# A retention and expert-mixture kernel: other slots for the remainder, the second-half units and some loads of tile 0, and another order of the last head units

## The chip, the cores and the metric

The kernel runs on one core of one Trainium2 chip. The metric is the device time of one execution in microseconds. The five engines are named as in the profile: PE (TensorE, with PEld for its weight loads), DVE (VectorE), ACT (ScalarE), POOL (GpSimd) and SP (SyncE, which only issues DMAs here).

## The reference

First a causal linear attention (retention) with 8 batches, 8 heads, 576 positions, head size 64:

```python
scores = (1/sqrt(64)) * q @ k^T
Dmat[h, i, j] = gamma[h] ** (i - j)  if i >= j else 0
attn = (scores * Dmat) @ v                      # (8, 8, 576, 64)
x = attn.transpose(0, 2, 1, 3).reshape(4608, 512)
```

Then a mixture of 4 experts over the 4608 rows, D = 512, F = 1024:

```python
p = domain_probs / (domain_probs.sum(-1) + 1e-9)
out = sum over e of  p[:, e] * (relu(x @ w1[e]) @ w2[e])
```

## The kernel before

**The decay** is split into a factor on k and a factor on q, so that each attention step is: cast q, k, v to bf16 with the factors, transpose q and k, scores on PE, the triangular mask on DVE (`sT`), a running sum of k^T v for the earlier chunks (`kv` on PE, then `sbd`), and values: first the products of the own chunk (`v` with `sT`), then the carried products (`sbd` with q).

**Attention of batch 0** is done ahead of everything else, in four `Unit`s `us[0]` to `us[3]` (half of the 512 positions, half of the heads; units 0 and 1 give rows p = 0, 1 of `xt`, units 2 and 3 rows p = 2, 3). Their transposes run on PE (`trans_pe`, L503) and are copied by ACT (L505). `scores` is L526 on PE and L528 on DVE, `kv` L545 on PE and L564 on ACT, `values` L575 (own) and L582 (carried) on PE and L598 on ACT. `warm(n)` issues n products of zeros (L140) on PE.

**Tile 0** follows: the rows 0 to 511. Its experts are walked in turn, 4 groups of up products (`up_group`, L345, 8 matmuls of 128x512, Relu on ACT, L349) and 4 of down products (`down_plain`, L364, 8 matmuls; every second one is read by DVE, L374 or L376, into an accumulator `acc0` and, for the last expert, stored by SP). That is 32 groups, numbered 0 to 31. After group n the functions listed in `slots[n]` are issued, in the order in which they were added. Expert e has its up groups in slots 8e to 8e+3 and its down groups in 8e+4 to 8e+7.

In these slots stand the work of the coming tiles:

- `remainder(slots, 0, ...)`: positions 512 to 575 of batch 0 (`Rem`): cast on DVE (L307, L309), two DMA transposes on the SP queue (L318, `kTr`, `qTr`), scores (L324 on PE, L325 on DVE), values (L330, L332 on PE, L336 on ACT). They write tile 1's `xt`.
- four second-half units `vs[0]` to `vs[3]`, batch 1, again `Unit`s: `v_cast` casts k and q on DVE (L492) and v on ACT (L488) and issues two DMA transposes on SP (`trans_dma`, L511, into `qkT`); `v_head` is scores and kv; then values. `qkT` and `sT` have two buffers each (`atp`, `bufs=2`), so the transposes of unit 2 wait until unit 0's values have read theirs, and those of unit 3 for unit 1.
- loads on the SP queue: `load_p` (the mixing weights of tile 1, `pB`), `load_pair` (batch 2, first pair, `raw1`), `load_rem(1)` (remainder of batch 1, `rawr`).
- `w_sum(which, lo, hi)` on DVE (L385 to L391): sums of the w2 weights, used from tile 1 on, where a fast form of the down products needs 7 instead of 8 partial products. `which` 1 overwrites a part of `wx[0]`, the w2 of experts 0 and 1.

The weights and the raw q, k, v of the second-half units are loaded on POOL's queue in a fixed order: w1(0) in halves, w2(0), w1(1), w2(1), remainder, w1(2), w2(2), units 0 and 1, w1(3), unit 2, w2(3), and unit 3 from inside `v_cast(0)`. `raws[3]` is the same buffer as `raws[0]`. `wx` holds w2, `w` w1.

**Tiles 1 to 8** have 16 up groups and 14 products each, with the attention of batch t + 1 in the slots of tile t; the remainder of batch 1 is cast in slot 0 of tile 1.

**PSUM** is one ring of four buffers of two banks; each `ring_tile` takes a free one, and waits for the readers of what was in it. The order of the instructions on each engine is the order in which the program issues them. Every engine works its own queue in order, and so do the DMA queues' issuers.

Of the kernel before, what the change touches and what calls it, by code (L numbers as in the profile page):

```python
# [23 lines left out]
def kernel(  # L24
# [10 lines left out]
    nc = tc.nc  # L35
    B, H, S, D = q.shape
    N, E = moe_domain_probs.shape
# [3 lines left out]
    C = 128  # L41
# [24 lines left out]
    def ring_tile(name, shape, dt=FP32):  # L66
        return ring.tile(shape, dt, tag="ring", name=name)
# [5 lines left out]
    def load_pair(t, b, p, eng=nc.sync):  # L73
        for n, src in srcs:
            for j in range(2):
                eng.dma_start(out=t[n][:, :, j, :],
                              in_=src[b, 2 * p + j, 0:SM, :].rearrange("(c p) d -> p c d", p=C))

    def load_rem(b, eng=nc.sync):
        for j in range(2):  # L80
            for n, src in (("k", k), ("v", v)):
                eng.dma_start(out=rawr[n][64 * j:64 * j + 64, :, j, :],
                                  in_=src[b, j:H:2, SM:S, :].rearrange("g t d -> t g d"))
        eng.dma_start(out=rawr["q"][0:R, :, :, :].rearrange("t g j d -> t (g j) d"),
                          in_=q[b, :, SM:S, :].rearrange("h t d -> t h d"))
# [3 lines left out]
    raw1 = {n: const.tile([128, NC, 2, D], FP32, name=f"raw1_{n}") for n, _ in srcs}  # L89
# [11 lines left out]
    def load_w1(e, f=slice(0, F)):  # L101
        return nc.gpsimd.dma_start(out=w1_sb[e][:, :, f], in_=moe_w1[e][:, f].rearrange("(dc p) f -> p dc f", p=128))
# [10 lines left out]
    NU = 4  # L113
# [23 lines left out]
    def warm(n):  # L137
        w = ring_tile("w", [128, 512])
        for _ in range(n):
            nc.tensor.matmul(w, lhsT=zz[:, 0:128], rhs=zz, start=True, stop=True)  # L140
# [69 lines left out]
    def mixing_weights():  # L210
        nc.vector.tensor_reduce(psm, prb, axis=mybir.AxisListType.X, op=ADD)
        nc.vector.tensor_scalar_add(psm, psm, 1e-9)
        nc.vector.reciprocal(psm, psm)
        nc.vector.tensor_tensor(pn, prb[:, :, :].rearrange("p t e -> p e t"),
                                psm.unsqueeze(1).to_broadcast([128, E, NTT]), op=MULT)
        nc.sync.dma_start(out=pd[:, :].rearrange("e (p t) -> p e t", p=128), in_=pn)
# [3 lines left out]
    def load_p(t, e, eng):  # L220
        pB[t, e] = ppool.tile([128, NT], FP32, tag="pB", name="pB")
        eng.dma_start(out=pB[t, e], in_=pd[e:e + 1, t * NT:(t + 1) * NT].to_broadcast([128, NT]))  # L222
# [4 lines left out]
    def xt_of(t):  # L227
        if t not in xt:
            xt[t] = xpool.tile([128, NDC, NT], BF16, tag="xt", name="xt")
        return xt[t]  # L230


    class Pair:
# [46 lines left out]
        def values(self, following=None):  # L280
            b, p = self.b, self.p
            o = ring_tile("o", [128, SM])
            for c in range(1, NC):
                nc.tensor.matmul(o[:, c * C:(c + 1) * C], lhsT=sbd[:, p, c - 1, :], rhs=self.qkT[:, 0, c, :],  # L284
                                 start=(c == 1), stop=False, skip_group_check=True)
            if following is not None:
                following.scores()
                following.kv()
            for c in range(NC):
                for j in range(2):  # L290
                    nc.tensor.matmul(o[64 * j:64 * j + 64, c * C:(c + 1) * C], lhsT=self.bf["v"][:, c, j, :],  # L291
                                     rhs=self.sT[:, j, c, :], start=False, stop=(c == NC - 1), skip_group_check=True)
            n0 = b * S
            a = 0
            while a < SM:
                t = (n0 + a) // NT
                z = min(SM, (t + 1) * NT - n0)
                nc.scalar.activation(xt_of(t)[:, p, n0 + a - t * NT:n0 + z - t * NT], o[:, a:z], Copy)
                a = z
# [176 lines left out]
    class Unit:  # L476
# [89 lines left out]
                nc.vector.tensor_copy(self.carry[:, gs, :], kvp[:, :, 1, :])  # L566

        def values(self):
            o = ring_tile("o0", [128, 2, 2, 2 * C])
            for g in range(2):  # L570
                for r in range(2):
                    for a in range(2):
                        for j in range(2):
                            ar = slice(64 * a, 64 * a + 64)
                            nc.tensor.matmul(o[64 * j:64 * j + 64, a, g, 0:C], lhsT=self.bf("v")[ar, r, 2 * g + j, :],  # L575
                                             rhs=self.sT[ar, j, g, r, :], start=(g == 0 and r == 0), stop=False,
                                             skip_group_check=True)
            for g in range(2):
                for a in range(2):
                    n = 2 * self.hf + a  # L580
                    if n > 0:
                        nc.tensor.matmul(o[:, a, g, 0:C], lhsT=sbd[:, 2 * self.g + g, n - 1, :],  # L582
                                         rhs=self.qT(slice(0, 128), g, a), start=False, stop=True,
                                         skip_group_check=True)
            i0 = 2 * C * self.hf
            n0 = self.b * S + i0
            for g in range(2):
                p = 2 * self.g + g
                a = 0
                while a < 2:  # L590
                    t = (n0 + C * a) // NT
                    z = 2 if n0 + 2 * C <= (t + 1) * NT else a + 1
                    lo, hi = n0 + C * a - t * NT, n0 + C * z - t * NT
                    w = z - a
                    nat = lambda ap: ap.rearrange("p (a t r) -> p a r t", a=w, r=2)
                    src = lambda x, y: o[:, x:y, g, 0:C].rearrange("p a (r t) -> p a r t", r=2)
                    if hi <= NT:
                        nc.scalar.activation(nat(xt_of(t)[:, p, lo:hi]), src(a, z), Copy)  # L598
                    else:
                        m = (NT - lo) // 2  # L600
                        for tt, d0, u0, u1 in ((t, lo, 0, m), (t + 1, 0, m, C // 2)):
                            nc.scalar.activation(
                                xt_of(tt)[:, p, d0:d0 + 2 * (u1 - u0)].rearrange("p (t r) -> p r t", r=2),
                                o[:, a, g, 0:C].rearrange("p (r t) -> p r t", r=2)[:, :, u0:u1], Copy)
                    a = z

    bfv0 = lambda g: {(n, hf): bf0[n][:, hf, g] for n in "kqv" for hf in range(2)}
    us = [Unit(0, hf, g, raw0[u], bfv0(g)) for u, (hf, g) in enumerate(units0)]
# [7 lines left out]
    for u in range(NU):  # L616
        if u + 1 < NU:
            us[u + 1].cast("k", nc.vector)
            us[u + 1].cast("q", nc.vector)
            us[u + 1].cast("v", nc.gpsimd)  # L620
            if u + 1 in load_w1_at:
                load_w1(*load_w1_at[u + 1])
        us[u].scores()
        if u + 1 < NU:
            if u == 0:
                warm(4)
            us[u + 1].trans_pe(2 if u == 0 else 1)
        us[u].kv()
        if u == 0:
            warm(1)  # L630
        us[u].values()
    mixing_weights()
    raw1u = {n: raw1[n][:, :, :, :].rearrange("p c j d -> p (c j d)") for n in "kqv"}
    bf1 = [{}, {}]
# [49 lines left out]
    def remainder(slots, b, at):  # L684
        add = lambda i, f: slots.setdefault(i, []).append(f)
        x = Rem(b)
        l, c, s, o = at
        if b > 0:
            add(l, lambda: load_rem(b))
        add(c, lambda: x.cast(nc.vector))  # L690
        add(c, x.trans_dma)
        add(s, x.scores)
        add(o, x.values)
# [5 lines left out]
    slots = {}  # L699
    add = lambda i, f: slots.setdefault(i, []).append(f)  # L700
    add(0, mixing_weights0)
    add(1, later_decays)
    remainder(slots, 0, (-1, 13, 20, 21))

    def v_cast(u):
        vs[u].cast("k", nc.vector)
# [6 lines left out]
    def v_head(u):  # L713
        vs[u].scores()
        vs[u].kv()

    for u, (c, sc, o) in enumerate(((17, 26, 27), (18, 27, 28), (25, 28, 29), (26, 29, 30))):
        add(c, lambda u=u: v_cast(u))
        add(o, lambda u=u: vs[u].values())
        add(sc, lambda u=u: v_head(u))  # L720
    add(27, lambda: [load_p(1, e, nc.sync) for e in range(E)])
    add(28, lambda: load_pair(raw1, 2, 0))
    add(30, lambda: load_rem(1))
    for j, ats in enumerate(((22, 22, 23, 23), (24, 24, 25, 25), (28, 28, 29, 29), (30, 30, 40, 41))):
        for at, which in zip(ats, (3, 1, 2, 4)):
            add(at, lambda which=which, j=j: w_sum(which, 4 * j, 4 * j + 4))
    run(slots, -1)
# [12 lines left out]
    for t in range(1, n_nt):  # L740
        slots = {i - 32: f for i, f in slots.items() if i >= 32} if t == 1 else {}
        d = [Down(h, t, s) for s in range(2)]
        add = lambda i, f: slots.setdefault(i, []).append(f)
# [62 lines left out]
```

## Time and profile before

| what | value |
|---|---|
| median of 4 runs | 551.28 us (550.79 to 551.98) |
| the profiled execution | 551.12 us, its span 549.4 us |
| mean granted TensorE clock | 0.987 |
| PE busy | 533.1 us, 97% of the span |
| DVE busy | 366.1 us, 67% |
| ACT, POOL busy | 109.5 us and 94.0 us |
| DMA | 64.27 MB, mean 117 GB/s |

In the profile a group is written as line, engine, operation, output <- inputs, shapes. "Idle before <- releaser" is how long the engine stood before the instruction and what ended that. The span is cut into 40 slices; the busy share of a slice is given in tenths, and PEclk is the clock that TensorE was granted in tenths of full speed. Tile 0 lies between about 21 and 93 us, tile 1 follows.

### The profile page before, as it was taken

The page shows a single profiled execution, that of the slowest core. Times are in us where ns is not written, and L with a number is a line of the kernel's source. Part 1 is how long each engine was busy: PE and PEld are TensorE (multiplying, and loading weights), DVE is VectorE, ACT ScalarE, POOL GpSimd, SP SyncE. Part 2 cuts the span into 40 slices and gives each one's busy share as a digit, 9 for nine tenths or more (in the row PEclk, how much of TensorE's full clock was granted, in tenths as well). Part 3 has the DMA queues.
Part 4 walks back from the last instruction along what each step waited for, and adds up shares of the span by engine and source line. Part 5 has one row for each costly group of instructions (what it writes and reads, how often), then busy time and mean ns, then how long its engine had stood idle before and what let it go on. Part 6 is the DMA issues. An engine that isn't in the chain of part 4 may idle for free.

```text
span 549.4 us, 10253 instructions
## 1 busy us (share of the span) xinstructions
PE 533.1 (97%) x4252; PEld 341.4 (62%) x4292; DVE 366.1 (67%) x484; ACT 109.5 (20%) x251; POOL 94.0 (17%) x126
## 2 busy tenths in 40 slices
PE   8899799999999999999999999999999999999997
PEld 4544344448844785468646874588448854884486
DVE  5424278886568766886488648875787667556764
ACT  4623151112302221122111311122022200000010
POOL 5733000211111221121111021111121100000000
PEclk9899798999999999999999999999999999999999
DMA  9999947765437451665176526573564311010001
GB/s 242 207 213 248 242 36 199 155 141 133 113 85 163 115 142 50 151 147 144 55 130 160 131 85 109 122 170 86 99 140 108 82 58 38 20 60 19 1 24 53
DMA packets 148126, 64.27 MB, mean 117 GB/s; under 512 B 127248, under 2 KB 138896, under 8 KB 148080
## 3 DMA queue, kind: packets, MB, share of 16 engines
q1 hardware_dynamic: 137760, 44.22, 36.0%
q0 software_dynamic: 10176, 19.27, 15.9%
q8 instruction: 33, 0.54, 0.4%
q14 instruction: 13, 0.11, 0.1%
q10 hardware_dynamic: 144, 0.13, 0.1%
HBM read 53.56 MB, written 9.51 MB: 115 GB/s over the span
## 4 chain that ended last, share of the span: by engine, by line
PE 91%; DMA 4%; DVE 2%; ACT 2%; issue 1%; SPq 0%; DVEq 0%; ACTq 0%
PE ph L345 43%; PE pd L437 36%; PE po L364 5%; DMA qTr<-bfr_q 2%; DVE h L351 1%; PE kvp L261 1%; PE s L274 1%; PE o L291 1%; DMA qkT<-bf_q 1%; ACT qkT L505 1%; DMA raw_0q<-in_q_dram 1%; DMA qkT<-q 1%; PE o L284 1%; ACT sbd L564 0%; PE pt L503 0%
## 5 line engine op out<-in xcount | busy, mean ns | idle before, releaser
L345 PE MATMUL ph<-xt,w 128*128 128x512 bf16 x1119 | 252.8, 380 | 3.1 <-DVE h L351 1.2
L345 PEld LDWEIGHTS <-w 128*128 128x128 bf16 x1152 | 111.4, 98 | 131.0 <-issue 2.4
L351 DVE SCALAR_TENSOR_TENSOR h<-ph,pB 128x1024 bf16<-128x1024 f32 x128 | 155.6, 1221 | 50.2 <-PE ph L345 49.8
L437 PEld LDWEIGHTS <-h 128*128 128x128 bf16 x1024 | 99.1, 98 | 14.2
L437 PEld LDWEIGHTS <-s 128*128 128x128 bf16 x768 | 74.6, 98 | 9.2
L437 PE MATMUL pd<-wx,h 128*128 128x256 bf16 x512 | 61.3, 273 | 0.0
L437 PE MATMUL pd<-wx,s 128*128 128x256 bf16 x512 | 61.2, 273 | 0.0
L222 POOL DMA_DIRECT2D pB<-pd x28 | 15.9, 566 | 165.5 <-DVE h L351 134.1
L266 ACT ACTIVATE sbd<-kvp 64x256 bf16<-64x256 f32 x48 | 18.1, 378 | 105.9 <-PE kvp L261 105.6
L472 POOL TENSOR_TENSOR ob<-v,p 128x256 f32<-128x256 f32 x15 | 10.9, 725 | 150.2 <-DVE v L469 93.5
L364 PE MATMUL po<-wx,h 128*128 128x512 bf16 x122 | 32.6, 418 | 0.6 <-issue 0.2
L276 DVE TENSOR_TENSOR sT<-s,tri 128x1024 bf16<-128x1024 f32 x24 | 29.2, 1216 | 2.2 <-PE s L274 2.2
L245 POOL TENSOR_TENSOR bf_q<-raw_q,gq 128x512 bf16<-128x512 f32 x24 | 26.2, 1092 | 25.8 <-DMA raw_q<-in_q_dram 20.9
L437 PE MATMUL pd<-t2w,s 128*128 128x256 bf16 x256 | 30.6, 273 | 0.0
L437 PE MATMUL pd<-t4w,h 128*128 128x256 bf16 x256 | 30.6, 273 | 0.0
L437 PE MATMUL pd<-t3w,h 128*128 128x256 bf16 x256 | 30.6, 273 | 0.0
L454 DVE TENSOR_TENSOR u<-pd,p 128x256 f32<-128x256 f32 x16 | 6.8, 424 | 34.7 <-PE pd L437 34.7
L445 ACT ACTIVATE p<-pd 128x256 f32<-128x256 f32 x16 | 6.1, 383 | 95.0 <-PE pd L437 84.0
L309 POOL TENSOR_TENSOR bfr_q<-rawr_q,gqr 64x512 bf16<-64x512 f32 x7 | 12.2, 1741 | 72.6 <-DMA out_dram<-acc 43.9
L364 PEld LDWEIGHTS <-h 128*128 128x128 bf16 x128 | 12.9, 105 | 16.5 <-issue 4.3
L456 DVE TENSOR_TENSOR oa<-pd,u 128x256 f32<-128x256 f32 x16 | 6.8, 424 | 23.8 <-PE pd L437 23.8
L418 DVE TENSOR_TENSOR s<-h,s 128x1024 bf16<-128x1024 bf16 x32 | 22.5, 743 | 0.0
(141 smaller groups left out, 400.6 us busy)
## 6 DMA issues: line engine op xcount, KB each, us to landing
pB<-pd POOLq DMA_DIRECT2D x28, 256.0 KB, 3.9
raw_k<-in_k_dram SPq DMA_DIRECT2D x48, 128.0 KB, 2.8
raw_q<-in_q_dram SPq DMA_DIRECT2D x48, 128.0 KB, 3.1
raw_v<-in_v_dram SPq DMA_DIRECT2D x48, 128.0 KB, 3.8
wx<-in_moe_w_dram POOLq DMA_DIRECT2D x4, 1024.0 KB, 16.5
out_dram<-oa SPq DMA_DIRECT2D x16, 256.0 KB, 2.1
out_dram<-ob SPq DMA_DIRECT2D x15, 256.0 KB, 2.0
w<-in_moe_w_dram POOLq DMA_DIRECT2D x3, 1024.0 KB, 15.5
```

The lines of the kernel that those rows point to most:

```text
L222: eng.dma_start(out=pB[t, e], in_=pd[e:e + 1, t * NT:(t + 1) * NT].to_broadcast([128, NT]))
L245: nc.gpsimd.tensor_tensor(self.bf["q"], raw["q"], gq[:, :, 2 * p:2 * p + 2].unsqueeze(3).to_broadcast([128, NC, 2, D]), op=MULT)
L266: nc.scalar.activation(sbd[r, self.p, :, r], kvp[r, :, :], Copy)
L276: nc.vector.tensor_tensor(self.sT[:, :, :, :].rearrange("p j c t -> p (j c) t"), s[:, :, :, :].rearrange("p j c t -> p (j c) t"), tri[:, : ...
L309: q_engine.tensor_tensor(bfr["q"][0:R], rawr["q"][0:R], gqr[0:R].rearrange("p (g j) -> p g j", j=2).unsqueeze(3).to_broadcast([R, NP, 2, D ...
L345: nc.tensor.matmul(ph[:, f, :], lhsT=w1_sb[e][:, dc, fc * 128:(fc + 1) * 128], rhs=x[:, dc, :], start=(dc == 0), stop=(dc == NDC - 1))
L351: nc.vector.scalar_tensor_tensor(h[:, fk:fk + 2, :], ph, 0.0, pB[t, e][:, :].unsqueeze(1).to_broadcast([128, 2, NT]), op0=MAX, op1=MULT)
L364: nc.tensor.matmul(po[:, g, :], lhsT=h[:, e * NFC + fc, ns * 128:(ns + 1) * 128], rhs=wx[e // 2][:, (e % 2) * NFC + fc, :, :].rearrange("p ...
L418: nc.vector.tensor_tensor(self.alloc("s4")[:, l], h[:, r, self.a], self.s2[:, l], op=SUB)
L437: mm = nc.tensor.matmul(dst, lhsT=src[:, kk, tok], rhs=rhs(c), start=(start and c == 0), stop=(c == KH - 1), skip_group_check=True)
L454: rd.append(nc.vector.tensor_tensor(self.u, Y, self.p1, op=ADD))
L472: nc.gpsimd.tensor_tensor(self.ob[:, HF:Dm], self.v, self.p5, op=ADD)
```

## The change

The change touches the order of the batch 0 units and the slots of tile 0.

- `values` is split into `values_own` and `values_carried`. For the units 0, 1 and 3 both are called one after the other as before (`trans_pe` and `kv` stay where they were). For unit 2, unit 3's scores and kv are issued between them, and three `warm` products behind its carried values.
- The remainder's scores go from slot 20 to 24, its values from 21 to 25.
- The casts and transposes of the second-half units 2 and 3 go from slots 25 and 26 to 24 and 25. Heads and values stay.
- `load_p` goes from slot 27 to 26, `load_pair` for batch 2 from 28 to 27, `load_rem(1)` from 30 to 27, which is ahead of the first two stores of `acc0`.
- The first two quarters of the `w_sum` steps go from slots 22 to 25 to slots 18 to 21.

```diff
         def values(self):
-            o = ring_tile("o0", [128, 2, 2, 2 * C])
+            self.values_own()
+            self.values_carried()
+
+        def values_own(self):
+            o = self.o = ring_tile("o0", [128, 2, 2, 2 * C])
             for g in range(2):
 ...
+        def values_carried(self):
+            o = self.o
             for g in range(2):
 ...
-        us[u].scores()
-        if u + 1 < NU:
+        if u < NU - 1:
+            us[u].scores()
             if u == 0:
                 warm(4)
             us[u + 1].trans_pe(2 if u == 0 else 1)
-        us[u].kv()
+            us[u].kv()
         if u == 0:
             warm(1)
-        us[u].values()
+        us[u].values_own()
+        if u == NU - 2:
+            us[u + 1].scores()
+            us[u + 1].kv()
+            us[u].values_carried()
+            warm(3)
+        else:
+            us[u].values_carried()
 ...
-    remainder(slots, 0, (-1, 13, 20, 21))
+    remainder(slots, 0, (-1, 13, 24, 25))
 ...
-    for u, (c, sc, o) in enumerate(((17, 26, 27), (18, 27, 28), (25, 28, 29), (26, 29, 30))):
+    for u, (c, sc, o) in enumerate(((17, 26, 27), (18, 27, 28), (24, 28, 29), (25, 29, 30))):
         add(c, lambda u=u: v_cast(u))
         add(o, lambda u=u: vs[u].values())
         add(sc, lambda u=u: v_head(u))
-    add(27, lambda: [load_p(1, e, nc.sync) for e in range(E)])
-    add(28, lambda: load_pair(raw1, 2, 0))
-    add(30, lambda: load_rem(1))
-    for j, ats in enumerate(((22, 22, 23, 23), (24, 24, 25, 25), (28, 28, 29, 29), (30, 30, 40, 41))):
+    add(26, lambda: [load_p(1, e, nc.sync) for e in range(E)])
+    add(27, lambda: load_pair(raw1, 2, 0))
+    add(27, lambda: load_rem(1))
+    for j, ats in enumerate(((18, 18, 19, 19), (20, 20, 21, 21), (28, 28, 29, 29), (30, 30, 40, 41))):
```

## The prediction

> **What bounds the kernel now.** The page comes first. TensorE (PE) is busy 97% of 549.4 us and holds 91% of the chain that ended last; the clock row shows where the rest is. (PEclk is the granted clock in tenths, 40 slices of 13.7 us.)
>
> ```profile
> PE   8899799999999999999999999999999999999997
> PEclk9899798999999999999999999999999999999999
> ```
>
> Slices 2, 5 and 7 (13.7 to 27, 55 to 69, 82 to 96 us) dip. All lie in the attention of batches 0 and 1 and in tile 0, where the change is. From 110 us on PE is busy 54.6 of every 55 us, so the whole gain or loss must come from the first 110 us. Next, the PE timeline from 48 to 112 us; in brackets the idle time before an instruction, and who ended it.
>
> ```profile
> 61.51 0.37 PE L324 MATMUL sr<-qTr,kTr 128*128 128x64 bf16 x4 [3.37 <-DMA qTr<-bfr_q]
> 61.70 3.60 PE L364 MATMUL po<-wx,h 128*128 128x512 bf16 x8
> ...
> 75.06 0.42 PE L526 MATMUL s<-qkT 64*64 64x128 bf16 x16
> ...
> 83.12 0.42 PE L526 MATMUL s<-qkT 64*64 64x128 bf16 x16 [1.30 <-DMA qkT<-q]
> ...
> 84.37 3.19 PE L364 MATMUL po<-wx,h 128*128 128x512 bf16 x7 [0.23 <-issue]
> ```
>
> So PE stands 3.37 us in slot 20 (remainder scores, for their DMA transpose) and 1.30 us in slot 28 (scores of second-half unit 2). After each wait products are slow: 8 in 3.60 us, 7 in 3.19 us, where undisturbed they take 0.216 each (24 in 5.18, by the chain). The windows view gives the reason (stretch, length, PE, PEld, DVE, ACT, POOL busy, then granted clock, DMA share, GB/s).
>
> ```profile
> 60.33:63.74 3.41, 2.23 (x9) 0.96 (x10) 0.42 (x1) 0.00 (x0) 0.00 (x0) 0.50 1.23 193
> 63.74:67.16 3.42, 3.42 (x16) 1.49 (x15) 1.82 (x3) 0.38 (x1) 0.00 (x0) 0.50 1.17 256
> ...
> 80.81:84.22 3.41, 2.03 (x53) 1.30 (x52) 0.63 (x1) 0.76 (x2) 0.00 (x0) 1.00 0.55 77
> 84.22:87.64 3.42, 3.27 (x15) 1.06 (x18) 2.77 (x6) 0.00 (x0) 0.00 (x0) 0.50 0.56 177
> ```
>
> Clock 0.50 comes in whole stretches of 3.41 us, following a stretch in which PE was busy 2.03 of 3.41. A stall thus costs itself and 1.7 us for each such stretch behind it: 3.37 + about 2.8 in slot 20, 1.3 + 1.7 in slot 28.
>
> Last, the DMA issues and what they compete with (packets and MB per queue, 60 to 62 us).
>
> ```profile
> q0 software_dynamic: 297, 0.30, 94.8%
> q1 hardware_dynamic: 295, 0.07, 33.0%
> ```
>
> The SP queue's transposes (q1) get one small packet for each packet of POOL's loads (q0), so they crawl while weights load. SP issued unit 0's q transpose at 53.00, and it landed 18.5 us later, as the DMA issues tell:
>
> ```profile
> qkT<-bf_q SPq DMA_TRANSPOSE x1, 18.5
> ```
>
> That is 71.5 us, absolute. Unit 1's landed at 71.8 (57.59 + 14.2) and 72.2 (60.93 + 11.3). In the run before nobody waits for them, because head 0 (L526, slot 26) comes at 75.06. This decides the case.
>
> **The head.** Before: own values of unit 2 end at 16.97, PE waits 0.76 us for sbd (ACT until 17.68), unit 3's scores start at 17.95, sT ends at 19.65, own values of unit 3 run 19.69, and the first up products are held until 21.52. After: scores 3 start when qkT lands (ACT, 17.02), at 17.06; kv, 1.14 by its row, to 18.6; carried 2 to 18.8; three warm products (3 x 0.213) to 19.45; sT is ready at 18.8, since its 1.22 us on DVE starts 0.9 sooner. Own 3 then starts at 19.45, but its xt copies stand behind sbd (0.77) and unit 2's copies (0.77) on ACT, until 20.15. The up product that waited until 21.52 starts near 20.75: 0.75 us. The built order gives unit 3's own values the buffer of its scores, read by the same sT, so no wait is added; a wait for unit 2's copies would take this back. If the clock is full from 19.38 (it was 0.50 to 22.79, with 1.27 us of products in it: 0.63 lost), 1.4 us in all; the bound below is half clock for one more stretch, -1 us. I take 1.4, but it is not in the sum: it is spent waiting in slot 26.
>
> **Slots 20 and 21 to 24 and 25.** Both remainder steps issue on PE, the mask on DVE and one copy on ACT; none passes a DMA. Four down groups from 54.85 (56.25 - 1.4) at 1.73 end at 61.8; group 24 at 63.5. qTr landed at 61.38, so the 3.37 us wait and the half-speed stretches are gone: about 6.2 us, gross. Groups 25 and 26 with sr and or (0.35) bring PE to head 0 at 67.3, not 75.06: 7.8 us early. What is late next is unit 0's q transpose, 71.5 in the old run.
>
> **When that lands (bounded, the decisive term).** Its queue starts earlier: the remainder cast on DVE (47.42) follows a down group's acc and moves 1.4 us with PE; the unit casts follow the next acc and raw loads that landed at 48.3 to 51.8. A start 1.5 us earlier gives 70.0. From below, PE's own arrival, 67.3: the packets equal in number put the transpose well ahead of the tail, and at 70 to 71 us the DMA share is only 0.05 although unit 0's landing is still to come. From above, 71.5, unchanged, if the tail of POOL's loads sets it. I take 70.0, nearest to the row that moves with its issue.
>
> **From there.** PE idles 2.7 us, so by the windows it runs at half clock afterwards. Head 0 to the end of unit 0's values took 3.41 us (75.06 to 78.47); at half, with scores and kv near 1.3, the group 8 x 0.43 and values 0.7, 5.4. They end at 75.4, 3.1 sooner than 78.47. Unit 2's transposes need qkT's buffer from unit 0 and follow 4.5 us later as before (78.47 to 82.99), so the 1.3 us wait in slot 28 stays, at 80.0. If half clock lasts into the work before it, that work covers the wait and the 1.7 us stretch behind it goes as well; I take 0.7 of it. ACT: unit 3's v cast now stands in slot 25 before group 26's Relu, and its raw_v landed at 71.3 (54.83 + 16.5). Cast 0.62, Relu 1.02, sbd 0.78: unit 0's values can't end before 74.0, beside 75.4, no cost here; with an early transpose it is the bound.
>
> A rule of the Trainium skill bears on this. Row first: 1.30 us of waiting (0.23 more near it) in 80.81 to 84.22 gave a whole stretch at 0.50. "TensorE: Matmul & The Clock Gate", section "Why this matters for your kernels", allows gaps up to about 3 us. By that rule the moved stall would cost no half clock and the change would be worth an estimated 2 us more (5.4 less 3.41); by the row it does cost it.
>
> **DVE, SP, POOL.** The eight w_sums of slots 18 to 21 (8 x 0.69 = 5.5 us) go from 66.7-76.5 into DVE's wait of 8.56 us before 61.92, and wx of expert 2 landed at 47.4: nothing. Uncovered, they would hold acc and sT by up to 5.5. load_p and load_pair are behind unit 3's transposes on SP anyway (issued from 84.40 on without a gap), so a slot sooner is nothing. load_rem passes two acc stores (2.10 us): rawr lands 2.1 sooner, and the stores 3.3 later, whose only reader is the output. Bounds: 0, if other loads slow it; 1.0, DVE's wait for rawr_k at 97.60. I take the 0.5 us that PE waited for a q transpose at 108.26, the last link. The casts of units 2 and 3, one slot sooner, wait for raw until 69.0 (52.60 + 16.4) at the latest, ahead of unit 0's sT on DVE: nothing. Their transposes wait for qkT as before. Tiles 1 to 8 are unchanged.
>
> Sum: 3.1 + 0.7 + 0.5 = 4.3 us. The profiled execution's 551.12 (1.7 outside its span) becomes 546.8; the median of the runs, 551.28, becomes 547.0.
>
> **Rivals.** (A) The transpose lands about when PE comes, 67.3 to 69. The ACT chain then sets values at 74.0, or 72.5 if raw_v comes 1.5 sooner (its issue waited 1.49 for ACT): 4.5 to 6.0, the slot 28 stretch up to 1.7, and 0.5: about 6.3, 545.0. For it: the equal packets; against: raw loads still end near 70. (B) The tail is unchanged, 71.5: values end at 76.9, 1.6 + 0.1 + 0.5 = 2.2, 549.1. For it: DMA share above 1 from 50 to 70 us, whatever is asked first. (C) All is handed back: landing near 73.0 and values at 78.4, 551.0. (D) Slower: the earlier remainder and unit transposes collide with more of POOL's big loads and the q transpose lands later than before. It decides from 73.5; at 75, values end at 80.4, 1.9 late, less 0.5: 552.7. Against it: the same bytes are in the queues, and DMA idles from 72 us in the old run.
>
> **How the numbers follow.** About 0.2% (1.1 us) can be told from no change. Forecast (3 to 5.3 us) 0.42, A 0.30, B 0.17, C 0.06, D 0.05: faster 0.89, same 0.06, slower 0.05. C and D and a thin end of A stay outside the range: 544.3 (A with full ACT gain, most of the stretch) to 549.6 (B with a little less).
>
> **What would show it.** Right: no wait before sr (L324); an idle time of 1 to 4 us before head 0's scores, ended by DMA qkT; clock 0.50 behind it; unit 0's q landing 69 to 71.5; up products from 20.7; no wait near 108. Wrong: sr still waiting, own values of unit 3 held past 20, DVE or ACT rather than a DMA in front of head 0, or a difference behind tile 1.

## The result, and the profile after

The changed kernel takes 549.55 us (median of 53 runs, 547.74 to 552.37), the kernel before 551.05 us (78 runs, 548.43 to 553.91): ratio 0.9974, interval [0.9967, 0.9981]. By the ratio that is 1.4 us faster [1.0, 1.8]; the forecast was 4.3 us faster (547.0), so the sign was right and the size was not. The first profiled execution of the changed kernel, 552.37 us, is the slowest of its 53. So the page below is that execution's, and the stage readings come from a second profiled execution of the same kernel (e0 below), 549.91 us (span 548.2), which is near the median. Ratios here and below leave out executions more than 1.5% above the fastest of the same kernel, which are three of f3's 12 and no others; their intervals are 95%.

The page's two rows after, of the first execution, in 40 slices of 13.8 us:

```profile
PE   7999958999999999999999999999999999999997
PEclk9999978999999999999999999999999999999999
```

The dips of slices 2 and 5 are gone. Slice 6 (69 to 83 us) now dips to 0.5 of PE, and slice 7 as before. Behind it nothing has changed. The chain that ended last says what stands there; PE held 91% and DMA 4% of it before.

```profile
PE 83%; DMA 11%; SPq 2%; DVE 1%; POOL 1%; issue 1%; ACT 1%; DVEq 0%
PE ph L345 41%; PE pd L437 36%; DMA qkT<-bf_q 4%; DMA wx<-in_moe_w_dram 3%; DMA rx<-in_q_dram 2%; SPq L119 2%; DVE h L351 1%; PE kvp L261 1%; PE po L364 1%; PE s L274 1%; DMA raw_3v<-in_v_dram 1%; PE o L291 1%; DMA qkT<-q 1%; PE o L284 1%; PE kvp L545 0%
```

The remainder's transpose (`qTr`, 2% before) has left the chain; unit 0's q transpose (`qkT<-bf_q`, 4%, 1% before) has taken its place, with loads ahead of its issue (`wx` 3%, `rx` 2%). The PE timeline of the second execution, from 48 us on:

```profile
55.27 4.91 PE L364 MATMUL po<-wx,h 128*128 128x512 bf16 x21
...
63.90 0.28 PE L324 MATMUL sr<-qTr,kTr 128*128 128x64 bf16 x4
...
72.63 0.55 PE L526 MATMUL s<-qkT 64*64 64x128 bf16 x16 [4.76 <-DMA qkT<-bf_q]
72.91 1.12 PE L545 MATMUL kvp<-bf_v,bf_k 64*64 64x64 bf16 x16
73.96 0.61 PE L345 MATMUL ph<-xt,w 128*128 128x512 bf16 x1
74.78 2.15 PE L345 MATMUL ph<-xt,w 128*128 128x512 bf16 x6 [0.22 <-issue]
...
82.18 0.42 PE L526 MATMUL s<-qkT 64*64 64x128 bf16 x16 [1.33 <-DMA qkT<-q]
82.40 0.84 PE L545 MATMUL kvp<-kv 64*64 64x64 bf16 x16
83.57 3.09 PE L364 MATMUL po<-wx,h 128*128 128x512 bf16 x7 [0.33 <-issue]
...
106.74 0.40 PE L274 MATMUL s<-qkT 64*128 64x128 bf16 x8
```

No wait is left before the remainder's scores (L324). PE comes to head 0 at 67.87 and stands 4.76 us there; 3.37 us in slot 20 have become 4.76 us in slot 26. Slot 28 is unchanged (1.33 us, then 7 products in 3.09). The wait before tile 1's scores (L274), 0.51 us at 108.26, is gone. Against the trace before: unit 2's scores 0.94 us earlier (82.18, 83.12), L274 1.52 us earlier (106.74, 108.26). The windows view shows the price behind the wait, in the same columns as before:

```profile
67.05:70.46 3.41, 0.82 (x4) 0.20 (x2) 0.00 (x0) 0.20 (x1) 0.00 (x0) 1.00 0.89 201
70.46:73.87 3.41, 1.24 (x32) 1.08 (x32) 2.03 (x3) 1.34 (x2) 0.00 (x0) 0.84 0.91 88
73.87:77.29 3.42, 3.20 (x29) 1.33 (x28) 0.86 (x2) 1.26 (x4) 0.00 (x0) 0.66 0.00 0
```

PE is busy 0.82 and 1.24 of 3.41 us, and the clock falls from the second stretch on (0.84, 0.66). These stretches are cut where it suits the table; the half clock itself is one stretch of 3.41 us, 72.77 to 76.19 (0.50 there). And the transpose itself, in the DMA issues:

```profile
qkT<-bf_q SPq DMA_TRANSPOSE x1, 20.1
```

SP issued it at 52.44 (53.00 before), and it landed 20.1 us later (18.5 before), at 72.5 instead of 71.5.

### The profile page after: what moved, and what is told of

It is laid out like the page before. It is cut to its first block, busy times and chain, and to the rows that moved or that the text cites. A ratio compares the mean times of both kernels' runs of the same rounds, so it can differ in the third digit from the quotient of the medians.

```text
span 550.7 us, 10257 instructions
## 1 busy us (share of the span) xinstructions
PE 532.0 (97%) x4255; PEld 340.4 (62%) x4295; DVE 364.4 (66%) x484; ACT 108.9 (20%) x251; POOL 93.5 (17%) x126
## 4 chain that ended last, share of the span: by engine, by line
PE 83%; DMA 11%; SPq 2%; DVE 1%; POOL 1%; issue 1%; ACT 1%; DVEq 0%
PE ph L345 41%; PE pd L437 36%; DMA qkT<-bf_q 4%; DMA wx<-in_moe_w_dram 3%; DMA rx<-in_q_dram 2%; SPq L119 2%; DVE h L351 1%; PE kvp L261 1%; PE po L364 1%; PE s L274 1%; DMA raw_3v<-in_v_dram 1%; PE o L291 1%; DMA qkT<-q 1%; PE o L284 1%; PE kvp L545 0%
## 5 line engine op out<-in xcount | busy, mean ns | idle before, releaser
L437 PEld LDWEIGHTS <-h 128*128 128x128 bf16 x1024 | 99.1, 98 | 14.2
L364 PE MATMUL po<-wx,h 128*128 128x512 bf16 x124 | 29.9, 392 | 0.9 <-DMA wx<-in_moe_w_dram 0.3
L309 POOL TENSOR_TENSOR bfr_q<-rawr_q,gqr 64x512 bf16<-64x512 f32 x7 | 10.9, 1551 | 72.6 <-DMA out_dram<-acc 42.6
L349 ACT ACTIVATE h<-ph 128x1024 bf16<-128x1024 f32 x16 | 16.3, 1020 | 31.3 <-PE ph L345 30.0
```

The costliest lines, as they stand in the source:

```text
L309: q_engine.tensor_tensor(bfr["q"][0:R], rawr["q"][0:R], gqr[0:R].rearrange("p (g j) -> p g j", j=2).unsqueeze(3).to_broadcast([R, NP, 2, D ...
L349: nc.scalar.activation(h[:, fk:fk + 2, :], ph, Relu)
L364: nc.tensor.matmul(po[:, g, :], lhsT=h[:, e * NFC + fc, ns * 128:(ns + 1) * 128], rhs=wx[e // 2][:, (e % 2) * NFC + fc, :, :].rearrange("p ...
L437: mm = nc.tensor.matmul(dst, lhsT=src[:, kk, tok], rhs=rhs(c), start=(start and c == 0), stop=(c == KH - 1), skip_group_check=True)
```

## The experiments

| kernel | what it is | median us | ratio to before | interval |
|---|---|---|---|---|
| e0_changed_again | the changed kernel | 549.80 | 0.9970 | [0.9956, 0.9985] |
| e1_head_only | the units' order alone | 550.65 | 0.9992 | [0.9981, 1.0004] |
| e2_slots_only | all slots, old order of units | 549.17 | 0.9966 | [0.9946, 0.9986] |
| e3_remainder_back | changed, remainder at 20, 21 | 549.48 | 0.9975 | [0.9961, 0.9988] |
| f1_loads_only | the three loads alone | 549.57 | 0.9976 | [0.9962, 0.9989] |
| f2_loads_back | changed without the three loads | 550.27 | 0.9988 | [0.9973, 1.0003] |
| f3_changed_less_load | changed, one 1 MB load less | 548.08 (542.30 to 551.30) | 0.9917 | [0.9887, 0.9947] |
| f4_before_less_load | before, the same load less | 553.73 | 1.0048 | [1.0030, 1.0066] |
| g1_pe_transposes | changed, units 0, 1 transposed on PE | 543.80 | 0.9859 | [0.9837, 0.9881] |
| g2_clock_filler | changed, products to fill the wait | 548.94 | 0.9968 | [0.9947, 0.9989] |
| g3_pe_transposes_cast_later | g1, unit 3's cast in slot 27 | 545.85 | 0.9900 | [0.9875, 0.9925] |
| g4_heads_later | changed, heads one slot later | 549.70 | 0.9969 | [0.9953, 0.9985] |
| h1_before_pe_transposes | before, units 0, 1 transposed on PE | 551.54 | 1.0006 | [0.9991, 1.0022] |
| h2_unit1_pe_transpose | changed, only unit 1 on PE | 548.22 | 0.9943 | [0.9924, 0.9962] |
| h3_slots_pe_transposes | e2 and g1 together | 544.62 | 0.9880 | [0.9862, 0.9898] |

The kernel before had medians of 550.83 beside the e runs, 551.08 beside f, 551.58 beside g and 551.34 beside h.

**Which part brings the 1.4 us?** The changed kernel was run again, and cut into the order of the units (e1) and the slots (e2).

> The changed kernel once more, for a typical trace. Theory 1 (the wait has moved: unit 0's q transpose on SP lands at the end of POOL's load stream, at an absolute time, and PE only waits for it at another place): 1.0 to 2.0 us below before; a wait of 3 to 6 us before head 0's scores (L526), released by DMA qkT, no wait before sr, landing within 1 us of the last raw_v. Theory 2 (a moved step blocks an engine: the v cast ahead of a Relu on ACT, or DVE's casts): the wait before head 0 is below 2 us, and an ACT or DVE wait ends last at unit 0's values.

> Only the order of the batch 0 units and the three warm products are changed; all slots as before. Theory 1: first up products 0.7 to 1.4 us sooner, and slot 20 waits that much longer for qTr; within 0.4 us of before. Rival (the head is a gain of its own): 1.0 to 1.4 us faster.

> Only the slots of tile 0 are changed; the head as before. Theory 1: the head's gain is spent in the wait at head 0, so this is within 0.4 us of the whole change, 1.0 to 2.0 below before, with a wait at head 0 shorter by 0.7 to 1.4. Rival (head and slots add up): half of the gain or less.

e0 met its theory 1: 1.65 us below before by the ratio, a wait of 4.76 us that a DMA ends, none before L324, and the landing at 72.5, together with the last raw load of POOL's queue (`raw_v` of unit 3, 72.5).

The slot edits, undone in e1, and made in the kernel before in e2:

```diff
-    remainder(slots, 0, (-1, 13, 20, 21))
+    remainder(slots, 0, (-1, 13, 24, 25))
-enumerate(((17, 26, 27), (18, 27, 28), (25, 28, 29), (26, 29, 30))):
+enumerate(((17, 26, 27), (18, 27, 28), (24, 28, 29), (25, 29, 30))):
-    # load_p, load_pair, load_rem in slots 27, 28, 30
+    # load_p, load_pair, load_rem in slots 26, 27, 27
-((22, 22, 23, 23), (24, 24, 25, 25),
+((18, 18, 19, 19), (20, 20, 21, 21),
```

The order of the units alone is worth nothing that can be told from no change, the slots alone as much as the whole change (the wait at head 0 in e2's trace, 5.42 us, is not shorter, which its theory had said; that trace is of one of its two slowest executions). In e1 the remainder's wait stands where it stood and takes what the head gives:

```profile
61.82 0.37 PE L324 MATMUL sr<-qTr,kTr 128*128 128x64 bf16 x4 [4.66 <-DMA qTr<-bfr_q]
```

It was 3.37 us in the trace before (and 4.28 in that of f1 below, which has the old order).

**Is it the remainder's place?** In the changed kernel, only this is undone:

```diff
-    remainder(slots, 0, (-1, 13, 24, 25))
+    remainder(slots, 0, (-1, 13, 20, 21))
```

> The whole change, but the remainder's scores and values back in slots 20 and 21. Theory 1: PE waits 3 to 5 us for qTr in slot 20, and the wait at head 0 shrinks to 0 to 2 us; the time goes back to within 0.5 us of before. Rival (the other slots, w_sum and loads make the gain): it stays 1 us or more below before.

It is not, and theory 1 of this run is wrong, its rival right. Slot 20 waits again (4.69 us for qTr), head 0 comes at 75.17 without a wait, and the time is that of the changed kernel, 549.48. The forecast's mechanism, a wait of some 6 us gross taken from slot 20, moves nothing that can be told.

**Is it the loads?** f1 makes only these edits in the kernel before, f2 undoes only these in the changed one:

```diff
-    add(27, lambda: [load_p(1, e, nc.sync) for e in range(E)])
-    add(28, lambda: load_pair(raw1, 2, 0))
-    add(30, lambda: load_rem(1))
+    add(26, lambda: [load_p(1, e, nc.sync) for e in range(E)])
+    add(27, lambda: load_pair(raw1, 2, 0))
+    add(27, lambda: load_rem(1))
```

> The kernel before with one part of the change alone: load_p, load_pair and load_rem(1) at slots 26, 27, 27. Theory 1b (the two waits of tile 0 only change places, what the change gains is the load of the next remainder ahead of two stores): 0.8 to 1.5 us below before, the wait for a q transpose near 107 us (0.5 to 1.2 us) gone, the wait in slot 20 still there. Rival (the gain is in slots 20 to 28): within 0.4 us of before.

> The whole change with the three loads back at slots 27, 28 and 30. Theory 1b: within 0.5 us of before, a wait of 0.3 to 1.2 us near 107 us. Rival (the gain is in slots 20 to 28): 1 to 2 us below before.

By the ratios, the loads alone give 1.3 us [0.6, 2.1], as much as the change; without them 0.7 us is left [-0.2, 1.5]. So the `w_sum` steps, the casts of units 2 and 3 and the remainder's place bring nothing that can be told beside the loads, though the first two were not run alone. The wait that they remove is this, as f2's PE timeline has it:

```profile
107.51 0.40 PE L274 MATMUL s<-qkT 64*128 64x128 bf16 x8 [0.74 <-DMA qkT<-bf_q]
```

In f1 PE came there at 106.16, and stood for nothing. With the loads at their old slots the traces show 0.51 (before), 0.74 (f2), 0.84 (h1), 1.18 (e1) and 1.21 us (f4); with the loads sooner none in the changed kernel's two traces, e3, f1, g1 to g4 and h2, 0.27 in h3, 0.37 in e2, 0.63 in f3. The chain behind it: DVE's remainder cast (L307) stood 1.02 us for `rawr_k` before, 1.10 in f2 and 2.06 in e1; with the sooner loads it started at 95.55 (e0) instead of 97.60. This chain names `load_rem`; the three loads were not run apart.

**Is it the load on the DMA queues that sets the landing?** Expert 3's w2 isn't loaded in f3 and f4; POOL clears its half of the buffer instead, so the products of expert 3 use zeros.

```diff
-    load_w2(3)
+    nc.gpsimd.memset(wx[1][:, NFC:2 * NFC, :, :], 0.0)
```

> The changed kernel without the load of expert 3's w2 (1 MB of POOL's queue); a memset of zeros on POOL stands in its place, so expert 3 adds nothing to the output. Theory 1 (the landing of the transposes at the end of POOL's loads sets head 0): landing of unit 0's q 4 us sooner or more, the wait before head 0 below 1.5 us, 4 to 7 us below before. Rival (the transposes are late of themselves, or ACT sets values): wait and time within 1 us of the changed kernel.

> The kernel before without the load of expert 3's w2, zeros by memset in its place (expert 3 adds nothing). Theory 1: the wait in slot 20 is for an earlier transpose that lands before that load is served, and stays at 2.5 to 4 us; 0 to 1.5 us below before, so that with less to load the change is worth 4 us or more. Rival: it gains as much as the changed kernel does without this load.

The kernel before became slower by 0.48% with 1 MB less to load, which neither theory said. In its trace PE stands 8.11 us for qTr:

```profile
65.40 0.37 PE L324 MATMUL sr<-qTr,kTr 128*128 128x64 bf16 x4 [8.11 <-DMA qTr<-bfr_q]
```

The transpose took 16.6 us from issue to landing, against 11.8 before and 12.8 to 13.3 in the other traces with the old slots (f1, e1, h1). Its queues from 60 to 62 us:

```profile
q0 software_dynamic: 105, 0.34, 56.3%
q1 hardware_dynamic: 310, 0.07, 50.1%
```

The one-for-one of before (297 and 295) isn't there, the transposes got no more packets through (310), and their packets took 50.1 / 310 against 33.0 / 295, 1.44 times as long each. POOL's queue (q0) moved no less in these 2 us (0.34 MB against 0.30), since unit 3's raw loads, in larger packets, now stand where the weight's load was. But from 62 to 70 us it sent 100 packets, 825 before, and even then the transposes sent fewer than before, 1115 against 1718. So fewer packets on the other queue didn't let them through sooner.

A landing 4 us sooner, as theory 1 had it for f3, isn't in either trace: unit 0's q landed at 71.0 in f4 and at 74.4 in f3. f3 is 4.6 us below before by its ratio, as theory 1 had it, but its executions range from 542.3 to 551.3 us, and the one trace is of the slowest (551.3: qTr 16.4 us, a wait of 1.02 us in slot 24 and 2.22 at head 0), so it doesn't tell what the others gained by. The clearing on POOL (3.53 us) also delays unit 3's loads (`raw_v` issued at 55.71 in f4, 53.90 in f1), and wasn't separated from the missing load. So whether the amount of load sets the landing isn't settled by these two, nor why the packets are slower, nor why f3's executions differ so much.

**Is it the clock behind the wait, or the wait?** g2 puts 16 products, whose result nobody reads, ahead of head 0:

```diff
     def v_head(u):
+        if u == 0:
+            w = ring_tile("w", [128, 512])
+            for _ in range(16):
+                nc.tensor.matmul(w, lhsT=w1_sb[0][:, 0, 0:128], rhs=w1_sb[0][:, 0, 0:512], start=True, stop=True)
         vs[u].scores()
```

> The changed kernel with 16 idle products (on a loaded w1, result unused) ahead of head 0's scores, 3.45 us at full clock, which fill most of the wait. Theory (the clock behind the wait costs 1.7 us or more): clock 1.00 behind head 0, 1 to 2.5 us below the changed kernel. Rival (the wait behind it in slot 28 takes back what the clock gives): within 0.5 us of the changed kernel.

```profile
73.32 0.42 PE L526 MATMUL s<-qkT 64*64 64x128 bf16 x16 [2.00 <-DMA qkT<-bf_q]
...
83.07 1.67 PE L364 MATMUL po<-wx,h 128*128 128x512 bf16 x7 [0.16 <-issue]
```

The clock stayed at 1.00 through it, and 7 products behind slot 28 took 1.67 us, not 3.09. From head 0's scores to unit 3's took 12.04 us (73.32 to 85.36), in e0 14.64 (72.63 to 87.27): the half clock, one stretch behind head 0 and one behind slot 28, costs 2.6 us there. But the landing was at 73.2 and not at 72.5 in this trace, and over 12 runs, 8 of them within 548.20 to 549.25 and 4 within 551.35 to 553.74, the median can't be told from the changed kernel's. Why the executions fall into two groups isn't known, so what a filler is worth stays open.

**Can the heads move to the landing?** g4 issues head 0 to 3 and their values one slot later.

```diff
-enumerate(((17, 26, 27), (18, 27, 28), (24, 28, 29), (25, 29, 30))):
+enumerate(((17, 27, 28), (18, 28, 29), (24, 29, 30), (25, 30, 31))):
```

> The changed kernel with heads and values of the four second-half units one slot later. Theory 1: PE does group 27 (1.73 us) inside the wait, which falls from 4.4 to 5.9 us to 2.7 to 4.2; unit 3's values then stand right ahead of tile 1 and cost up to 0.9 us: 0 to 1.5 us below the changed kernel. Rival (the landing moves with PE): the wait stays as it was, and the time is 0 to 1 us above.

Head 0 waits 3.30 instead of 4.76 us, to 73.14, and the time is unchanged: the work behind it is later instead (unit 2's scores at 83.20, 82.18 in e0).

**Is it the DMA transposes of units 0 and 1?** g1 makes them on PE, in slots 22 and 23, copied by ACT, as the kernel does for batch 0.

```diff
-    ident = epool.tile([128, 128], BF16)
+    ident = const.tile([128, 128], BF16, name="ident")
 ...
-        vs[u].trans_dma()
+        if u > 1:
+            vs[u].trans_dma()
 ...
+    add(22, vs[0].trans_pe)
+    add(23, vs[1].trans_pe)
```

> The changed kernel, but the transposes of the second-half units 0 and 1 are done on PE and copied by ACT (slots 22 and 23, 16 products in all), not by DMA; the identity matrix is kept for it. Theory 1 (PE stands in slot 26 for unit 0's DMA transpose and runs at half clock behind that): the wait of 4.4 to 5.9 us before head 0 and the stretch behind it go, for 1.6 us of products: 4 to 6.5 us below the changed kernel, 5 to 8 below before. Rival (ACT's v cast, held by raw_v, sets unit 0's values): the wait goes to unit 0's own values, 0 to 2 us below the changed kernel.

543.80 us, 7.8 below the kernel before, the best version here. Its PE timeline:

```profile
60.20 0.39 PE L503 MATMUL pt<-ident,bf_k 128*128 128x128 bf16 x4
60.42 0.39 PE L503 MATMUL pt<-ident,bf_q 128*128 128x128 bf16 x4
...
64.54 0.28 PE L324 MATMUL sr<-qTr,kTr 128*128 128x64 bf16 x4
...
68.44 0.42 PE L526 MATMUL s<-qkT 64*64 64x128 bf16 x16
...
76.75 0.42 PE L526 MATMUL s<-qkT 64*64 64x128 bf16 x16 [1.55 <-DMA qkT<-q]
...
101.11 0.40 PE L274 MATMUL s<-qkT 64*128 64x128 bf16 x8
```

Two groups of four transposes take under 0.8 us on PE for each unit, and no wait is left until unit 2's scores; L274 comes 5.6 us sooner than in e0. The raw loads behind them land sooner too: ACT stands 1.23 us for `raw_v` of unit 3, in e0 5.28.

h1 makes g1's edits in the kernel before, h3 makes them in e2, and h2 leaves unit 0 on the DMA queue in the changed kernel:

```diff
-        if u > 1:
+        if u != 1:
             vs[u].trans_dma()
 ...
-    add(22, vs[0].trans_pe)
     add(23, vs[1].trans_pe)
```

> The kernel before with units 0 and 1 transposed on PE (slots 22 and 23). Theory 1 (the wait in slot 20 and the wait at head 0 only change places while the DMA transposes are there): the wait for qTr in slot 20 stays at 2.5 to 5 us and nothing waited at head 0, so 0 to 2 us below before, and the change is worth 5.5 to 8 us once both kernels have PE transposes. Rival (the PE transposes are a gain of their own): 4 us or more below before.

> Slots of the change and PE transposes of units 0 and 1, but the head as before. Theory 1 (the head's time was spent in the wait): with the wait gone the head counts, 0.7 to 1.5 us above the kernel with the whole change and PE transposes. Rival (ACT's v cast, waiting for raw_v, absorbs it again): within 0.4 us of that kernel.

> The changed kernel with unit 1 alone transposed on PE; unit 0's two DMA transposes stay as issued. If all four together set the landing: unit 0's q lands 2 to 4 us sooner (68 to 70), the wait at head 0 is 1 to 3 us, and the time 2 to 5 us below the changed kernel. If its own place among POOL's packets sets it: landing and wait within 1 us of the changed kernel, and the time within 1 us.

In the kernel before it is worth nothing (551.54): PE stands 4.83 us in slot 20 for the remainder, and head 0 comes at 76.97, later than the DMA transpose landed in any trace. That is theory 1 of h1. So the two waits are halves of one thing: the other slots alone only uncover unit 0's transpose, and taking that transpose away only helps once the slots have moved. Both together give 7.8 us. h3's median is 0.8 us above g1's, which would be the order of the units, counting when no wait behind it takes it back; but the intervals overlap, with 5 and 4 executions, and both traces reach L274 at 101.11, so that isn't shown. h2's trace bears on what sets the landing:

```profile
70.38 0.42 PE L526 MATMUL s<-qkT 64*64 64x128 bf16 x16 [2.07 <-DMA qkT<-bf_q]
```

Unit 0's q transpose, still a DMA and issued at 52.32, landed 17.9 us later, in e0 20.1. With unit 1's two transposes left out, though they are issued after it, it went 2.2 us faster than there, and 0.6 us faster than in the fastest of the traces that have them and the full load (18.5, before). This is one trace. The wait (2.07 us) and the landing (70.2) are as the first theory had them; the time fell by about 1.5 us (0.9943 against 0.9970), a little less than its 2 to 5.

g3 is g1 with unit 3's cast in slot 27 instead of 25, so that unit 2's transposes would have ACT and DVE to themselves.

```diff
-enumerate(((17, 26, 27), (18, 27, 28), (24, 28, 29), (25, 29, 30))):
+enumerate(((17, 26, 27), (18, 27, 28), (24, 28, 29), (27, 29, 30))):
```

> As the kernel with PE transposes, and unit 3's casts from slot 25 to 27, behind the Relus of groups 26 and 27 on ACT. Theory: where raw_v lands last, this takes ACT's wait of up to 2 us out of the way of unit 0's values: 0.5 to 2 us below the kernel with PE transposes alone. Rival (raw_v has landed by then): within 0.4 us of it.

Both theories missed: the median is 2 us above g1's, though the intervals just overlap. Unit 2's wait fell from 1.55 to 1.06 us, but unit 3's transposes are issued later, and its scores, which waited for nothing in g1, wait:

```profile
82.12 0.42 PE L526 MATMUL s<-qkT 64*64 64x128 bf16 x16 [2.33 <-DMA qkT<-q]
```

This trace is of the fastest of its six (544.36) and reaches L274 only 0.36 us later than g1's, so it doesn't account for the 2 us.

## Why the prediction was wrong in size

**The decisive term failed: "When that lands".** It took a landing of 70.0 with bounds of 67.3 and 71.5, because the row "moves with its issue". The issue moved 0.56 us and not 1.5 (53.00 to 52.44; the cast ahead of it 0.98 us, 50.87 to 49.89), and the time to the landing isn't a constant: 18.5 us in the one trace that was read, 19.6 to 21.0 in nine others with the same loads and transposes. The landing, issue and duration added, and beside it that of unit 3's `raw_v`, the last of POOL's loads:

| kernel | issue | to landing | landed | last raw load landed |
|---|---|---|---|---|
| before | 53.00 | 18.5 | 71.5 | 71.3 |
| f1, old order and slots | 52.38 | 19.6 | 72.0 | 71.7 |
| e1, new order, old slots | 52.34 | 19.7 | 72.0 | 72.0 |
| e3, e0, f2 | 52.19, 52.44, 52.70 | 19.9, 20.1, 19.7 | 72.1, 72.5, 72.4 | 71.8, 72.5, 73.1 |
| g4, g2 | 52.63, 52.43 | 20.4, 20.8 | 73.0, 73.2 | 73.1, 73.3 |
| after, e2 | 53.86, 54.40 | 21.0, 20.8 | 74.9, 75.2 | 75.1, 75.4 |
| f4, f3, less load | 52.44, 55.54 | 18.6, 18.9 | 71.0, 74.4 | 70.7, 74.2 |
| h2, without unit 1's | 52.32 | 17.9 | 70.2 | 71.8 |

With the full load and all the transposes none has it before 71.5, and the order of the units and the slots don't sort them: f1 and e1 land alike. The upper bound of the term, "71.5, unchanged", was the earliest that any of these showed. What goes with the landing is the end of POOL's loads: in all twelve traces with the transposes of both units the two lie within 0.7 us of each other. The prediction had both rows, 71.5 and 71.3, and took the landing to move with its own issue instead. In e0 ACT's line has the same moment:

```profile
72.53 0.63 ACT L488 ACTIVATE kv<-raw_v 128x512 bf16<-128x512 f32 x1 [5.28 <-DMA raw_v<-in_v_dram]
```

Which of the two holds the other isn't separated: with no transposes of units 0 and 1 (g1) `raw_v` took 14.8 us from issue to landing, in e0 18.3, and with unit 0's alone (h2) they no longer end together. In the first execution after the change, DVE's casts of unit 0 also waited for the raw loads themselves (0.93 us, until 51.73), which a sooner PE can't help. Rival B's mechanism, a landing at the tail of POOL's loads, is the one that the traces fit; and by h2 and g1 fewer DMA transposes are what helps.

**What followed from it.** The remainder's move was to bring 3.1 and 0.7 us; e3, which takes it back, can't be told from the changed kernel, and without the loads the change is worth 0.7 us [-0.2, 1.5] in all. In e0's trace the 3.1 us for unit 0's values became 0.94 us at unit 2's scores. The 0.7 us for the half clock behind slot 28 became 0.1 (3.09 against 3.19). Head 0 to the end of unit 0's values took 4.9 us in e0 (72.63 to 77.51), forecast 5.4. Rival B, tail unchanged, gave 549.1, and 549.55 was measured, at the upper end of the stated range. That it came so near is in part luck: it counted 1.7 us for the slots and 0.5 for the loads, where the runs have 0.7 [-0.2, 1.5] and 1.3 [0.6, 2.1]. Rival D, decided from a landing at 73.5, is what single executions show: with landings of 74.9 and 75.2, the traces of after and e2 belong to executions of 552.37 and 551.83 us (D's price for 75 was 552.7). But there POOL's loads are late too: `w1` of expert 3 was issued at 45.98 and 46.35, at 42.53 before and 43.60 in e0. Two smaller slips changed nothing: the raw loads of rival A end at 71.3 by the prediction's own row and not near 70, and the range's lower end, 544.3, holds 0.5 of the stretch's 1.7 us beside A's 6.0 and 0.5, not most of it.

**The loads were sized at 0.5 and are worth 1.3 [0.6, 2.1].** The step read the wait in one trace. In that trace slot 28's half clock had made PE late by 1.6 us (5.09 us from unit 2's to unit 3's scores, 3.46 in f1), and so covered a part of the wait. From unit 2's scores to L274 the traces with half clock there took 25.14 (before) and 25.37 (f2) with the old loads, 24.36 to 24.57 (e0, e3, g1, after) with the new: some 0.8 less. Without half clock they took 24.39 to 25.44 (h1, e1, f4) with the old and 23.47 to 24.09 (g2, f1, h3, e2) with the new: 1.3 less on average. That the gain of the change is this one alone isn't shown: e2, e3, f1 and e0 can't be told from each other, and f2's 0.7 us [-0.2, 1.5] leaves room for a part from the slots.

**The head's 1.4 was partly the clock of one trace.** The first down group starts at 28.62 before, 27.64 in e0 and 27.65 in e1, but at 27.69 in f1, which has the old order, at 28.28 in h3 and 29.42 in h1 (0.77 of it a new wait for `wx`). The order is worth 0 to 1 us there, and 0.8 us by the medians of g1 and h3, which is not clear of the noise. That it is "spent waiting in slot 26", or in slot 20 without the other edits, was right.

**Right as told:** no wait before L324 (in the changed kernel's two traces), an idle time before head 0 ended by DMA qkT, half clock behind it, slot 28's wait unchanged at 1.3, the L274 wait gone, up products from 20.7 (20.69 and 20.37), w_sums, load_p and unit casts at nothing, as far as runs that move them together with other parts can tell. PE's arrival was given as 67.3 and was 67.87; the wait was 4.76 and not 2.7 us. On the rule of the Trainium skill that was weighed ("TensorE: Matmul & The Clock Gate", section "Why this matters for your kernels", gaps up to about 3 us), the row was the better guide in this kernel too: 1.33 us of waiting was followed by 7 products in 3.09 us, though not in every kernel, as told below. Head 0's wait of 4.76 us is above the page's figure and doesn't tell the two apart.

## What to carry to other kernels

When a wait is taken away, ask what PE meets at its new, earlier place, and take the landing of that from several executions: a landing read as 18.5 us in one trace was 19.6 to 21.0 us in nine others, and the earliest of them was used as the latest. Look also at what else lands at that moment: here it was the last load of the other queue, every time. Two waits for the same crowded queue in a row are one problem, and should be costed together: the change alone gave 1.4 us, the PE transposes alone nothing, both 7.8. Small transposes that are needed soon, while weights stream in, can be worth doing on PE: here they cost under 0.8 us of PE and 1.02 us of ACT for each unit, where PE had stood 4.8 us.

## What the runs showed of the hardware that was not expected

- With 1 MB less to load, the kernel before got 2.65 us slower (551.08 to 553.73), and a DMA transpose took 16.6 instead of 11.8 to 13.3 us. From 60 to 62 us a transpose's packets took 1.44 times as long, though the other queue sent a third as many packets, if larger ones.
- A transpose already issued lands sooner when two transposes behind it are left out (17.9 us in h2, 18.5 to 21.0 in the ten traces with them and the full load). It is one trace.
- The same wait in slot 28 has two prices. With 1.27 to 1.55 us of waiting, unit 3's scores follow unit 2's by 5.0 to 5.1 us in the kernel before, the changed kernel's two traces, e3, f2 and g4, and by 4.9 in g1; with 1.11 to 1.43 us, by 3.5 us in e1, e2, f1, f3, f4, g2, h1 and h3. So the half clock costs about 1.5 us or nothing. Where the wait lies in the stretches of 3.41 us bears on it but doesn't decide it alone. PE was busy for 1.70 (g1) to 2.14 us (f2) of the stretch with the wait where half clock followed; in e1 and h3 the wait lies across two stretches (2.52 and 2.82 us in e1), and none followed. But f4 with 2.08, f1 with 2.10 and e2 with 2.15 us had none either, and e0 with 2.08 had it.
